# Attention followed by a squared-ReLU feed-forward layer on one core: a two-part start, another route for batch 2, smaller w_out units and another order of exps

## The chip, the cores and the metric

The kernel runs on one core of a Trainium2 chip. The metric is device time in microseconds (us) of one execution. The span that the profile shows is about 1.7 us shorter than that time, because it runs from the first to the last instruction.

## The reference

Eight batches of attention (8 heads, 576 tokens, 64 columns, 16 extra "beacon" keys and values ahead of the tokens, causal among the tokens), then a feed-forward layer over all 4608 tokens:

```python
scores = scale * np.matmul(q, concat([beacon_k, k]).transpose(0, 1, 3, 2))     # masked above the diagonal
a = exp(scores - max); a /= a.sum(-1) + 1e-09
x = np.matmul(a, concat([beacon_v, v])).transpose(0, 2, 1, 3).reshape(4608, 512)
h = x @ w_in                 # 512 x 2048
r = np.maximum(h, 0.0)
return (r * r) @ w_out       # 2048 x 512
```

Inputs and output are fp32; the kernel computes in bf16.

## The kernel before

A small list scheduler inside the kernel fixes, when the kernel is built, the order of instructions on every engine. It guesses durations, and the chip may be slower or faster, but the order stays: if TensorE reaches an instruction whose data is late, everything behind it waits. The same holds for SyncE, on whose queue most loads, all crossbar transposes and all stores stand.

Keys and queries must be transposed (head columns on the partitions). Batches below `NPE` are loaded and cast in one transfer by GpSimd and transposed by TensorE; the others are loaded in natural layout by SyncE, cast by GpSimd, and transposed by a DMA through the crossbar. The attention output `xn` must be transposed too: on TensorE for batches below `NXPE`, by five crossbar transposes on SyncE for the others.

```python
    NPE = 3
    NXPE = 2
    # ...
    def add_strided(b, prio):                     # q and k of batches 0 to 2
        after = [w_ops["in", 3]] if b == 1 else [strided[b - 1][HP - 1, "q"]] if b else []
        step = 1 if b == 0 else 2
        for pr in range(0, HP, step):
            h = slice(2 * pr, 2 * (pr + step))
            for n, (x, t, dst) in enumerate((("k", k, ks), ("q", q, qs))):
                # one load for all 576 tokens of these heads: 96 partitions x 6 tokens
                ... nc.gpsimd.dma_start(out=dst[b % 2][:, h],
                                        in_=t[b, h].rearrange("h (p s) d -> p h s d", s=NS))
    # ... 12 transposes of 96x96 for each pair of heads, for k and for q
    def add_trans(b, x, prio):                    # q or k of batches 3 to 7, on SyncE
        ... nc.sync.dma_start(out=dst[b % 2]..., in_=srcb[b % 2]..., transpose=True)
        deps = [cast[b, x, c] for c in range(NT)]
    # ...
                exps.append(add(..., "ACT", ..., prio=base + i + s, deps=[qk], give=(qk, s)))
    # ...
    def add_xt(b):                                # x of batches NXPE to 7, on SyncE
        for t in range(NT):
            ... nc.sync.dma_start(out=xT[:, :, at:at + n], in_=xn[b % 2][0:n, t, :], transpose=True)
    # ...
    def add_weights():                            # w_in in quarters, behind batch 0's v
            w_ops["in", i] = add(f"win{i}", "POOL", 1.3, emit, prio=-100 + i,
                                 sync=[v_loads[0][3]] if i == 0 else (),
                                 behind=[w_ops["in", i - 1]] if i else (), dma=3.15)
    # ...
            for half in range(2):                 # w_out: 16 matmuls of a 128-token tile in 2 units of 8
                prev = add(f"s2.{j}.{ts}.{half}", "PE", 1.73, emit_s2, ...)
    # ...
        if b < NXPE:
            add_xt_pe(b)
        else:
            add_xt(b)
```

The first batch's attention is split by tokens: the first 240 go through attention and the first w_in matmuls (width 240) before the other 336 (w_in width 272 for what is left of the first chunk of 512).

The softmax here doesn't subtract the row's maximum and nothing guards it: scores larger than these inputs give would overflow.

Of the kernel before, what the change touches and what calls it, by code (L numbers as in the profile page):

```python
# [179 lines left out]
def kernel(  # L180
# [29 lines left out]
    def sb(name, shape, dt):  # L210
# [13 lines left out]
          for i in range(2)]  # L224
    kb = [qk_area[:, (2 * i + 1) * W:(2 * i + 2) * W].rearrange("p (g c d) -> p g c d", g=HP, c=NT)
          for i in range(2)]
    qs = [qk_area[0:NP, (2 * i) * WS:(2 * i + 1) * WS].rearrange("p (h s d) -> p h s d", h=H, s=NS)
          for i in range(2)]
    ks = [qk_area[0:NP, (2 * i + 1) * WS:(2 * i + 2) * WS].rearrange("p (h s d) -> p h s d", h=H, s=NS)
          for i in range(2)]  # L230
    bkf = [sb("bkf", [Nb, H, D], FP32)] * 2
    bks = [sb(f"bks{i}", [Nb, H, D], BF16) for i in range(2)]
    vb = [sb(f"vb{i}", [128, NT, H, D + 1], BF16) for i in range(2)]
# [65 lines left out]
    def t_start(t):  # L299
        return max(0, 128 * t - Nb)  # L300

    NPE = 3
    NXPE = 2
    SOFT_V = (1,)
    zero_ops = {}
    strided = {}
# [66 lines left out]
    def add_beacon(b, prio):  # L373
        ld = add(f"bkl{b}", "SP", 0.65, lambda e: [nc.sync.dma_start(
            out=bkf[b % 2], in_=beacon_k[b].transpose([1, 0, 2]))], prio=prio, dma=0.1,
                 deps=[cast[b - 1, "bk"]] if b else [])
        cast[b, "bk"] = add(f"bkc{b}", "DVE", 0.4, lambda e: nc.vector.tensor_copy(bks[b % 2], bkf[b % 2]), prio=prio,
                               deps=[ld])
        return cast[b, "bk"]

    def add_strided(b, prio):
        loads = {}
        bk = add_beacon(b, prio)
        after = [w_ops["in", 3]] if b == 1 else [strided[b - 1][HP - 1, "q"]] if b else []
        free = trans[b - 2, "q"] + trans[b - 2, "k"] if b >= 2 else []
        trans[b, "q"], trans[b, "k"] = [], []
        step = 1 if b == 0 else 2
        for pr in range(0, HP, step):
            h = slice(2 * pr, 2 * (pr + step))
            for n, (x, t, dst) in enumerate((("k", k, ks), ("q", q, qs))):  # L390
                def emit(e, t=t, dst=dst, h=h):
                    return [nc.gpsimd.dma_start(out=dst[b % 2][:, h],  # L392
                                                in_=t[b, h].rearrange("h (p s) d -> p h s d", s=NS))]
                o = add(f"sld{b}{x}{pr}", "POOL", 0.65 * step, emit, prio=prio + pr + 0.1 * n, behind=after,
                        deps=free, dma=0.92 * step)
                for i in range(step):
                    loads[pr + i, x] = o
        strided[b] = loads
        for pr in range(HP):
            h = slice(2 * pr, 2 * pr + 2)  # L400
            box = {}

            busy = qk_ops[HP * (b - 2) + pr] if b >= 2 else []

            def emit_tp(e, x, pr=pr, h=h, box=box):
                pp = ps[box[x].held[2]].bitcast(BF16)
                t, at = (ks, Nb) if x == "k" else (qs, 0)
                if x == "k":
                    nc.tensor.transpose(pp[:, 0:Nb], bks[b % 2][:, h, :], ident[0:Nb, 0:Nb])  # L409
                for u in range(NS):  # L410
                    for hj in range(2):
                        nc.tensor.transpose(pp[64 * hj:64 * hj + 64, at + u * NP:at + (u + 1) * NP],  # L412
                                            t[b % 2][:, 2 * pr + hj, u, :], ident[0:NP, 0:NP])

            for n, x in enumerate("kq"):
                box[x] = add(f"tp{b}.{pr}{x}", "PE", 0.65 if b else 0.9, lambda e, x=x, f=emit_tp: f(e, x),
                             prio=100.0 * (HP * b + pr) - 190 + 0.1 * n,
                             deps=[bk if x == "k" else None, loads[pr, x], ident_op] + busy, take=("ps", "tp"))

            def emit_k(e, pr=pr, box=box):  # L420
                pp = ps[box["k"].held[2]].bitcast(BF16)
                copy_on(e, kT[b % 2][:, pr, 0:Nb], pp[:, 0:Nb])
                copy_on(e, kT[b % 2][:, pr, Nb:Nb + S].rearrange("p (n s) -> p n s", s=NS),
                        pp[:, Nb:Nb + S].rearrange("p (s n) -> p n s", s=NS))

            def emit_q(e, pr=pr, box=box):
                pp = ps[box["q"].held[2]].bitcast(BF16)
                copy_on(e, qT[b % 2][:, pr, 0:S].rearrange("p (n s) -> p n s", s=NS),
                        pp[:, 0:S].rearrange("p (s n) -> p n s", s=NS))

            ek = add(f"ek{b}.{pr}", "DVE", 0.85, emit_k, prio=-200.0, deps=[box["k"]], give=box["k"])
            eq = add(f"eq{b}.{pr}", ("DVE", "ACT"), 0.7, emit_q, prio=-199.0, deps=[box["q"]], give=box["q"])
            trans[b, "k"].append(ek)
            trans[b, "q"].append(eq)


    class Phase:

# [43 lines left out]
    def add_pair(b, pr):  # L482
        p = HP * b + pr
        qk_ops[p] = []

        def gate(o):
            if p < HP:
                return True
            return o.progress >= mlp_chunk_us * (LEAD + PACE * (p - HP))

        if b < NPE:
            qk_deps = [trans[b, "k"][pr], trans[b, "q"][pr]]
        else:
            qk_deps = trans[b, "k"] + trans[b, "q"]
        take_pt = add(f"pt{p}", "-", 0.0, None, prio=100.0 * p, deps=qk_deps, take=("pt", "pt"), gate=gate)
        av_ops[p] = []
        for n, ph in enumerate(phases(b)):
            add_phase(b, pr, p, n, ph, take_pt, qk_deps, gate)

    def add_phase(b, pr, p, n, ph, take_pt, qk_deps, gate):  # L500
        base = 100.0 * p + 1000.0 * n
# [2 lines left out]
        for i in range(0, len(ph.pieces), size):  # L504
# [22 lines left out]
            for s, (_, off, width) in enumerate(group):  # L527
                def emit_exp(e, off=off, width=width, box=box, s=s):
                    st = strips[box["qk"].slots[s]]
                    nc.scalar.activation(pt[take_pt.held[2]][:, :, off:off + width], st[:, :, 0:width],  # L530
                                         AF.Exp, bias=0.0, scale=scale)

                exps.append(add(f"exp{p}.{n}.{i + s}", "ACT", 0.18 + 2 * width / 1200.0, emit_exp,
                                prio=base + i + s, deps=[qk], give=(qk, s)))

        def emit_mask(e):
            P = pt[take_pt.held[2]]
# [111 lines left out]
    def add_weights():  # L649
        for i in range(4):  # L650
            def emit(e, i=i):
                w = d_ff // 4
                return [nc.gpsimd.dma_start(  # L653
                    out=w_in_sb[:, :, i * w:(i + 1) * w],
                    in_=moe_w_in.rearrange("(m p) f -> p m f", p=128)[:, :, i * w:(i + 1) * w])]
            w_ops["in", i] = add(f"win{i}", "POOL", 1.3, emit, prio=-100 + i, sync=[v_loads[0][3]] if i == 0 else (),
                                 behind=[w_ops["in", i - 1]] if i else (), dma=3.15)
    def add_weights_out():
        for i in range(4):
            def emit(e, i=i):  # L660
# [6 lines left out]
    def add_chunk(j):  # L667
# [52 lines left out]
            sq.append(sqs)  # L720
        for ts in range(TCH // 128):
            prev, first = None, {}
            for half in range(2):
                def emit_s2(e, ts=ts, half=half, first=first):
                    o = ps[first["s2"].held[2]]
                    for fc in range(8 * half, 8 * half + 8):
                        nc.tensor.matmul(o, G[:, fc, ts * 128:(ts + 1) * 128],  # L727
                                         w_out_sb[:, fc, :], start=(fc == 0), stop=(fc == NFT - 1))

                prev = add(f"s2.{j}.{ts}.{half}", "PE", 1.73, emit_s2, prio=base + 100 + 2 * ts + half,  # L730
                           deps=[x for f in range(4 * half, 4 * half + 4) for x in sq[f]]
                           + [w_ops["out", qd] for qd in (2 * half, 2 * half + 1)] + [prev],
                           take=None if half else ("ps", "mlp"), pe_time=1.73)
                first.setdefault("s2", prev)
            s2_ops[j, ts] = prev
            u = 2 * j + ts // 2
# [29 lines left out]
    late = []  # L766
    for b in range(B):
        lp = 10.0 * b
        if b < NPE:
            add_strided(b, lp - 200.0 if b == 0 else lp)  # L770
        if NPE <= b < NPE + 2:
# [2 lines left out]
        for n, (x, c) in enumerate(([] if b < NPE else nat) + [("v", c) for c in range(NT)]):  # L774
            behind, sync = [], []
            if x == "v" and b == 0:
                if c == 0:
                    sync = [strided[0][0, "q"]]
            elif x == "v" and b == 1 and c == 0:
                behind = [strided[1][HP - 1, "q"]]  # L780
            elif b == 2 and n == 0:
                sync = [w_ops["out", 3]]
            add_load(b, x, c, lp + 0.1 * n, behind, sync)
            if x == "v":
                v_loads[b].append(load_chain[-1])
        if b >= NPE:
            add_trans(b, "k", lp - 5.0)
            add_trans(b, "q", lp - 5.1)
        if b == 0:
            add_weights()  # L790
        if b == 1:
            add_weights_out()
        for pr in range(HP):
# [45 lines left out]
```

## Time and profile before

| | before |
|---|---|
| time, median of 3 | 351.12 us (350.99 to 351.77) |
| span in the profile | 349.6 us |
| TensorE busy | 335.9 us, 96% |
| first w_in matmul; first of width 272 | 26.47 us; 34.45 us |
| TensorE at half speed until | about 25.9 us |

These are lines of the page: the span, then each engine's busy time (PE is TensorE, PEld its weight loads, DVE VectorE, ACT ScalarE, POOL GpSimd).

```profile
span 349.6 us, 7413 instructions
PE 335.9 (96%) x2980; PEld 179.5 (51%) x2980; DVE 167.9 (48%) x391; ACT 197.3 (56%) x298; POOL 82.8 (24%) x132
```

The table of windows of the kernel before says where the other 4% lie. After the window's bounds and length come each engine's busy us with its instructions, the granted clock, the DMA engines' share and GB/s.

```profile
core 0: us, PE busy (x) PEld busy (x) DVE busy (x) ACT busy (x) POOL busy (x), PEclk, DMA share, GB/s
0.00:10.00 10.00, 3.73 (x59) 2.56 (x61) 5.66 (x25) 2.82 (x4) 6.82 (x18) 1.00 0.80 113
10.00:20.00 10.00, 7.83 (x97) 4.58 (x97) 5.92 (x20) 6.26 (x9) 3.81 (x6) 1.00 0.72 141
20.00:30.00 10.00, 9.70 (x141) 7.18 (x142) 7.87 (x34) 8.56 (x13) 6.03 (x9) 1.00 1.19 197
30.00:40.00 10.00, 9.18 (x161) 7.01 (x161) 7.14 (x19) 6.65 (x15) 4.77 (x8) 1.00 1.22 216
50.00:100.00 50.00, 50.00 (x567) 27.90 (x566) 32.41 (x75) 33.21 (x48) 17.57 (x30) 1.00 1.17 213
```

TensorE is the limit from 50 us on. It is idle in the first 20 us, where it has little data, and it is slow there too. The timeline of TensorE before shows the speed: start, duration, line, operation, output and inputs, and the number of matmuls. The same 12 attention-value matmuls take 0.84 us at 22.88 and 0.53 us at 27.04, although the clock column reads 1.00 in all the windows above.

```profile
22.88 0.84 PE L563 MATMUL ps<-vb,pt 128*128 128x65 bf16 x12
26.47 0.58 PE L692 MATMUL ps<-xT,w_in 128*128 128x240 bf16 x4
27.04 0.53 PE L563 MATMUL ps<-vb,pt 128*128 128x65 bf16 x12
34.45 1.10 PE L692 MATMUL ps<-xT,w_in 128*128 128x272 bf16 x8
```

The list of DMA issues of the kernel before in the first 50 us (KB each, median us from issue to landing) has the w_in quarters and the last v load of batch 0. Both are quick, since w_in is issued when v has landed.

```profile
w_in<-in_moe_w_in_dram POOLq DMA_DIRECT2D x4, 512.0 KB, 8.3
stg<-in_v_dram SPq DMA_DIRECT2D x1, 160.0 KB, 4.8
```

```profile
152.18 1.03 PE L692 MATMUL ps<-xT,w_in 128*128 128x512 bf16 x4
```

That w_in work needs 320 tokens of batch 3, which are the first three of the five. The third is issued from about 148.15 on (145.57 and twice 1.29); with 2.5 us from the start of its issue to landing (measured below, in e4) it is there at about 150.6. So the kernel before has about 1.5 us in hand here. That is an estimate from these lines, and it was made only after the experiments.

### The profile page before, as it was taken

The page shows a single profiled execution, that of the slowest core. Times are in us where ns is not written, and L with a number is a line of the kernel's source. Part 1 is how long each engine was busy: PE and PEld are TensorE (multiplying, and loading weights), DVE is VectorE, ACT ScalarE, POOL GpSimd, SP SyncE. Part 2 cuts the span into 40 slices and gives each one's busy share as a digit, 9 for nine tenths or more (in the row PEclk, how much of TensorE's full clock was granted, in tenths as well). Part 3 has the DMA queues.
Part 4 walks back from the last instruction along what each step waited for, and adds up shares of the span by engine and source line. Part 5 has one row for each costly group of instructions (what it writes and reads, how often), then busy time and mean ns, then how long its engine had stood idle before and what let it go on. Part 6 is the DMA issues. An engine that isn't in the chain of part 4 may idle for free.

```text
span 349.6 us, 7413 instructions
## 1 busy us (share of the span) xinstructions
PE 335.9 (96%) x2980; PEld 179.5 (51%) x2980; DVE 167.9 (48%) x391; ACT 197.3 (56%) x298; POOL 82.8 (24%) x132
## 2 busy tenths in 40 slices
PE   3789999999999999999999999999999999999995
PEld 2458676645454455444445875454544444444442
DVE  6477886645762576237632864266413302301300
ACT  1686775657834876467646764577436515614611
POOL 7274640472353046105250440000000000000000
PEclk9999999999999999999999999999999999999999
DMA  7989999999998999969996999240015011011002
GB/s 101 185 139 204 220 206 210 217 234 191 230 202 143 215 253 204 187 141 233 218 229 97 220 259 155 86 113 16 2 60 129 0 60 60 2 60 61 2 13 107
DMA packets 137010, 49.50 MB, mean 142 GB/s; under 512 B 123344, under 2 KB 132048, under 8 KB 136976
## 3 DMA queue, kind: packets, MB, share of 16 engines
q1 hardware_dynamic: 127472, 40.09, 55.9%
q0 software_dynamic: 9504, 8.95, 15.7%
q8 instruction: 23, 0.38, 0.5%
q14 instruction: 11, 0.09, 0.1%
HBM read 37.22 MB, written 9.44 MB: 133 GB/s over the span
## 4 chain that ended last, share of the span: by engine, by line
PE 86%; DMA 9%; POOL 1%; SPq 1%; issue 1%; ACT 0%; POOLq 0%; ACTq 0%
PE ps L727 36%; PE ps L692 34%; PE ps L563 8%; PE strip L515 7%; DMA stg<-in_v_dram 5%; DMA qk_area<-in_k_dram 4%; SPq L331 1%; DMA qk_area<-in_q_dram 1%; POOL w_in L653 1%; PE ps L412 1%; POOL vb L286 0%; PE ps L628 0%; ACT osb L284 0%; POOL qk_area L392 0%; PE ps L409 0%
## 5 line engine op out<-in xcount | busy, mean ns | idle before, releaser
L692 PE MATMUL ps<-xT,w_in 128*128 128x512 bf16 (+3 forms) x704 | 134.4, 340 | 0.0
L727 PE MATMUL ps<-w_out,g 128*128 128x512 bf16 x576 | 130.5, 379 | 0.0
L530 ACT ACTIVATE pt<-strip 128x832 bf16<-128x832 f32 (+4 forms) x128 | 104.3, 863 | 37.3 <-PE strip L515 36.9
L708 ACT ACTIVATE g<-ps 128x512 bf16<-128x512 f32 (+2 forms) x126 | 70.3, 558 | 40.9 <-PE ps L692 39.8
L692 PEld LDWEIGHTS <-w_in 128*128 128x128 bf16 x704 | 65.1, 98 | 53.9 <-issue 2.5
L727 PEld LDWEIGHTS <-g 128*128 128x128 bf16 x576 | 54.2, 98 | 63.3 <-issue 1.2
L717 DVE TENSOR_TENSOR g<-g 128x1024 bf16<-128x1024 bf16 (+2 forms) x80 | 52.7, 661 | 59.3 <-ACT g L708 57.6
L284 ACT COPY osb<-ps 128x512 f32<-128x512 f32 x33 | 19.3, 585 | 57.8 <-PE ps L727 57.8
L563 PEld LDWEIGHTS <-pt 128*128 128x128 bf16 (+1 forms) x960 | 37.3, 99 | 17.0 <-issue 8.1
L286 POOL CAST qk_area<-stg 128x512 bf16<-128x512 f32 (+2 forms) x50 | 34.1, 695 | 42.9 <-DMA stg<-in_k_dram 21.6
L563 PE MATMUL ps<-vb,pt 128*128 128x65 bf16 (+1 forms) x960 | 42.6, 197 | 0.7 <-POOL vb L286 0.4
L286 POOL CAST vb<-stg 128x512 bf16<-128x512 f32 (+1 forms) x38 | 24.0, 646 | 66.0 <-DMA stg<-in_v_dram 22.7
L540 DVE TENSOR_TENSOR pt<-pt,tri 128x1024 bf16<-128x1024 bf16 (+1 forms) x36 | 23.9, 669 | 30.2 <-ACT pt L530 30.1
L515 PE MATMUL strip<-qT,kT 64*128 64x80 bf16 (+7 forms) x400 | 37.2, 293 | 0.1
L580 DVE TENSOR_TENSOR xn<-ps,rcp 128x320 bf16<-128x320 f32 (+2 forms) x72 | 32.7, 454 | 2.6
L579 DVE RECIPROCAL rcp<-ps 128x5 f32<-128x5 f32 (+2 forms) x72 | 13.4, 186 | 39.7 <-PE ps L563 39.3
L710 DVE TENSOR_SCALAR g<-ps 128x512 bf16<-128x512 f32 (+2 forms) x34 | 21.0, 620 | 16.9 <-PE ps L692 16.0
L515 PEld LDWEIGHTS <-kT 64*128 64x128 bf16 x400 | 12.9, 97 | 16.7 <-issue 12.7
L412 PE MATMUL ps<-ident,qk_area 96*64 96x96 bf16 x288 | 12.3, 234 | 4.0 <-DMA qk_area<-in_k_dram 2.3
L286 DVE COPY kT<-ps 128x16 bf16<-128x16 bf16 (+1 forms) x24 | 9.8, 454 | 6.8 <-PE ps L412 6.7
L412 PEld LDWEIGHTS <-qk_area 96*64 96x64 bf16 x288 | 8.9, 126 | 6.3 <-DMA qk_area<-in_k_dram 2.7
L544 DVE TENSOR_TENSOR pt<-pt,tri 80x160 bf16<-80x160 bf16 x32 | 10.4, 324 | 0.0
(33 smaller groups left out, 58.1 us busy)
## 6 DMA issues: line engine op xcount, KB each, us to landing
out_dram<-osb SPq DMA_DIRECT2D x17, 512.0 KB, 3.1
stg<-in_v_dram SPq DMA_DIRECT2D x21, 256.0 KB, 5.3
stg<-in_q_dram SPq DMA_DIRECT2D x20, 256.0 KB, 5.0
stg<-in_k_dram SPq DMA_DIRECT2D x15, 256.0 KB, 5.1
w_in<-in_moe_w_in_dram POOLq DMA_DIRECT2D x4, 512.0 KB, 8.3
w_out<-in_moe_w_out_dram POOLq DMA_DIRECT2D x4, 512.0 KB, 11.0
stg<-in_v_dram SPq DMA_DIRECT2D x7, 224.0 KB, 4.8
qk_area<-in_k_dram POOLq DMA_DIRECT2D x4, 288.0 KB, 12.3
```

Of the source, the lines that this page charges most:

```text
L286: eng[e].tensor_copy(dst, src)
L412: nc.tensor.transpose(pp[64 * hj:64 * hj + 64, at + u * NP:at + (u + 1) * NP], t[b % 2][:, 2 * pr + hj, u, :], ident[0:NP, 0:NP])
L515: nc.tensor.matmul(st[:, hj, at:at + t1 - t0], kT[b % 2][hp, pr, 128 * c:128 * c + 128], qT[b % 2][hp, pr, t0:t1], start=True, stop=True,)
L530: nc.scalar.activation(pt[take_pt.held[2]][:, :, off:off + width], st[:, :, 0:width], AF.Exp, bias=0.0, scale=scale)
L540: nc.vector.tensor_tensor(out=d, in0=d, in1=tri[:, m0:m0 + m, :][:, None].to_broadcast([128, 2, m, 128]), op=ALU.min)
L563: nc.tensor.matmul(a[:, (t - tl[0]) * (D + 1):(t - tl[0] + 1) * (D + 1)], P[0:rr, hj, o:o + 128], vb[b % 2][0:rr, c, h, :], start=(c == 0) ...
L580: nc.vector.tensor_tensor(out=xn[b % 2].rearrange("p t (h d) -> p t h d", d=D)[:, tl[0]:tl[0] + nt, h], in0=a[:, :, 0:D], in1=r[:, :, None ...
L692: nc.tensor.matmul(h[:, lo - spans[0][0]:hi - spans[0][0]], w_in_sb[:, mc, ft * 128:(ft + 1) * 128], xT[:, mc, lo % RING:lo % RING + hi - lo],
L708: nc.scalar.activation(dst, h, AF.Relu, bias=0.0, scale=1.0)
L710: nc.vector.tensor_scalar(out=dst, in0=h, scalar1=0.0, scalar2=None, op0=ALU.max)
L717: nc.vector.tensor_tensor(out=d, in0=d, in1=d, op=ALU.mult)
L727: nc.tensor.matmul(o, G[:, fc, ts * 128:(ts + 1) * 128], w_out_sb[:, fc, :], start=(fc == 0), stop=(fc == NFT - 1))
```

## The change

The intent is to fill the empty start and to take work from TensorE.

1. Batch 0's q and k are loaded in two parts (tokens 0 to 239, then the rest), with the first w_in quarter right behind the first part, and the other three behind the second. Three of v's five loads now wait for the first part.
2. Batch 2's q and k leave TensorE for the crossbar (`NPE` 3 to 2), and batch 2's x comes to TensorE in exchange (`NXPE` 2 to 3).
3. w_out is issued in units of 4 matmuls rather than 8.
4. On ScalarE, ready exps go ahead of ready relus.

```diff
+    whole_parts = [(0, NP, NS)]
+    parts_of = {0: [(0, 120, 2), (240, 112, 3)], 1: whole_parts, 2: whole_parts}
@@
-    NPE = 3
-    NXPE = 2
+    NPE = 2
+    NXPE = 3
@@ (add_part_loads is new; add_strided is rewritten to transpose and evict part by part)
+    def add_part_loads(b, part, prio, after, free):
+        t0, np_, ns = parts_of[b][part]
+        step = HP // 2
+        for pr in range(0, HP, step):
+            ...
+                    return [nc.gpsimd.dma_start(
+                        out=strided_buf(b, x, part)[:, h],
+                        in_=t[b, h, t0:t0 + np_ * ns, :].rearrange("h (p s) d -> p h s d", s=ns))]
@@
-                                prio=base + i + s, deps=[qk], give=(qk, s)))
+                                prio=(base + i + s) * 1.0e-4 - 30.0, deps=[qk], give=(qk, s)))
@@
-            w_ops["in", i] = add(f"win{i}", "POOL", 1.3, emit, prio=-100 + i, sync=[v_loads[0][3]] if i == 0 else (),
-                                 behind=[w_ops["in", i - 1]] if i else (), dma=3.15)
+            w_ops["in", i] = add(f"win{i}", "POOL", 1.3, emit, prio=-100 + i, behind=first_loads[min(i, 1)] if i < 2 else [w_ops["in", i - 1]], dma=3.15)
+            if i == 0:
+                first_loads.append(add_part_loads(0, 1, -95.0, [w_ops["in", 0]], []))
@@
-            for half in range(2):
+            for qd in range(4):
                 ...
-                    for fc in range(8 * half, 8 * half + 8):
+                    for fc in range(4 * qd, 4 * qd + 4):
@@
             if x == "v" and b == 0:
-                if c == 0:
-                    sync = [strided[0][0, "q"]]
+                if c == 2:
+                    sync = [strided[0, 0, HP - 1, "q"]]
```

Cut: the grouping of the 4 beacon transposes of a batch into one unit, and the bookkeeping of buffers.

## The prediction

> **What bounds the kernel.** TensorE: busy 335.9 of 349.6 us on the page (96%); the table of windows shows it 100% busy from 50 to 262 us and 83.86 of 84 us after that. Idle time lies at the start: 6.3 us in 0:10, 2.2 in 10:20, 1.5 in 20:50; the last 3.6 us are the final eviction and store. The start also runs at half speed: in the timeline 12 attention-value matmuls take 0.84 us at 22.9 us and 0.53 at 27.0; 12 q/k transposes 0.69 us at 10 us and 0.45 at 33.6. The switch falls at about 25.9 us. The Trainium skill ("TensorE: Matmul & The Clock Gate", Part 1) says the array starts at half clock until sustained activity releases it; the durations agree, though the page's clock row says 9 throughout.
>
> **What changes, with slots (start to start) from the timeline after 50 us.**
> - Batch 2's q/k leave TensorE: 8 groups of 12 transposes at 0.38 us plus 4 beacon transposes at 0.1: -3.4 us. Its x comes on: 4 groups of 5 at about 0.3 us: +1.3. Batch 0 has 16 transposes fewer: -0.5. My sum of all TensorE slots, with other small differences, falls from 328.1 to 326.0 us. All on the critical path.
> - w_out units of 4, and exps before relus, only reorder: a w_out matmul's slot is 0.216 us either way, and after 50 us there is no wait to remove. About 0.
> - Batch 2's q/k need 10 natural loads (256-byte rows, about 900 packets/us, 10.5 us), casts and two crossbar transposes of 5 to 7 us. Ready near 68 us; TensorE asks near 76. No stall.
> - Start. Before: w_in is issued at 18.1 behind the v loads, the DMA engines idle from 17 to 19.5, its first quarter lands at 26.5, and the first w_in matmul follows at once. After: tokens 0 to 239 are in by 9 us, w_in's first quarter by 13. But in TensorE's order the first w_in matmul stands behind all transposes of the second part, which queues behind that quarter and shares the DMA engines with v: landing 14 to 19 us (estimate). So first w_in matmul near 20 us. ScalarE then has 12 exps of 0.87 us plus copies, until about 29 us as before; TensorE fills with w_in work, half of it still at half clock.
>
> **Sum.** Before, the first w_in matmul of width 272 starts at 34.5 us. After, it stands 3.9 us of work deeper; I expect it at 36.8 us (34.5 to 38.5, by when the clock rises: 19, 22.5 or 26 us), with 304.6 + 3.6 us to follow. So the start gains 1.5 us, later waits 0.5 to 1, batch 2's exchange 2. Span about 345.5, time **347.0 us**, range 342.5 to 350.5. Faster by over 2% (below 344.2): 0.2; within 2%: 0.76; slower: 0.04.
>
> **What would show it.** First w_in matmul at 18 to 22 us; TensorE idle before 20 us still 6 to 8 us; half-speed durations until 22 to 26 us; last exp of batch 0 at 28 to 30 us; no TensorE idle from 50 to 340 us; batch 2's crossbar transposes landed before its first qk.
>
> **What would make it wrong.** A denser start may lift the clock at 19 us: 2 to 3 us better. The first part's 512-byte reads may be slower[...]: no gain at the start. Batch 2's crossbar transposes may land after 76 us, as all queues share 16 DMA engines ("DMA: Bandwidth & Descriptors", Issuing engines are not separate DMA queues; no run here shows it yet), and stall TensorE, whose order is fixed.

## More of the kernel before

The timeline of SyncE before, near 140 us, shows the crossbar transposes of batch 5's q and k and then of batch 3's x: each holds the queue for as long as its duration says. TensorE's timeline has the first w_in matmuls on that x.

```profile
137.55 4.16 SPq L363 DMA_TRANSPOSE qT<-qk_area  x1
141.80 3.68 SPq L363 DMA_TRANSPOSE kT<-qk_area  x1
145.57 6.44 SPq L611 DMA_TRANSPOSE xT<-xn  x5
```

## The result, and the profile after

Ratios are the mean time of one kernel's fast runs over that of the other's fast runs of the same rounds, so they are not quite the ratios of the medians quoted beside them.

| | before | after |
|---|---|---|
| time, median of 4 | 351.44 us (350.99 to 351.86) | 355.83 us (354.81 to 356.42) |
| ratio | 1 | 1.0122, 95% interval 1.0094 to 1.0151 |
| span in the profile | 349.6 us | 354.3 us |
| TensorE busy | 335.9 us | 331.6 us |
| first w_in matmul | 26.47 us | 21.76 us |
| first w_in matmul of width 272 | 34.45 us | 45.42 us |
| from there to the end | 315.2 us | 308.9 us |

The change made the kernel 1.2% slower; the prediction was 1.2% faster. The same views of the kernel after follow: the page, the waits of TensorE (what was waited for: us in total, times, longest), and the table of windows.

```profile
span 354.3 us, 7194 instructions
PE 331.6 (94%) x2846; PEld 176.9 (50%) x2884; DVE 172.9 (49%) x396; ACT 191.2 (54%) x287; POOL 89.2 (25%) x137
```

```profile
PE ps L725 <- DVE xT L292: 7.0, 1, 7.0
```

```profile
0.00:10.00 10.00, 1.86 (x24) 1.25 (x24) 4.47 (x24) 2.11 (x4) 8.74 (x19) 1.00 0.93 124
10.00:20.00 10.00, 9.15 (x114) 5.65 (x114) 8.14 (x30) 6.95 (x12) 6.62 (x10) 1.00 1.34 188
20.00:30.00 10.00, 2.99 (x31) 1.62 (x28) 1.12 (x5) 2.92 (x5) 3.25 (x4) 1.00 1.23 196
30.00:40.00 10.00, 10.00 (x136) 7.15 (x135) 8.00 (x25) 7.05 (x11) 6.59 (x10) 1.00 1.17 216
50.00:100.00 50.00, 49.45 (x440) 27.35 (x444) 30.04 (x66) 29.53 (x46) 19.56 (x27) 1.00 1.04 192
```

The window from 20 to 30 us is nearly empty on TensorE, VectorE and ScalarE, while the DMA engines are as busy as anywhere. The timelines of TensorE and then of VectorE after say why. In brackets stand the idle time before an instruction and what ended it.

```profile
21.76 0.78 PE L725 MATMUL ps<-xT,w_in 128*128 128x240 bf16 x3
29.55 0.36 PE L725 MATMUL ps<-xT,w_in 128*128 128x240 bf16 x1 [7.01 <-DVE xT L292]
31.01 0.84 PE L595 MATMUL ps<-vb,pt 128*128 128x65 bf16 x12
34.82 0.53 PE L595 MATMUL ps<-vb,pt 128*128 128x65 bf16 x12
45.42 1.10 PE L725 MATMUL ps<-xT,w_in 128*128 128x272 bf16 x8
```

```profile
28.88 0.43 DVE L292 CAST vb<-stg 80x512 bf16<-80x512 f32 x1 [8.95 <-DMA stg<-in_v_dram]
29.22 0.27 DVE L292 COPY xT<-ps 128x240 bf16<-128x240 bf16 x1
```

TensorE waits for a copy on VectorE, the copy stands in VectorE's fixed order behind the cast of the last v tile, and that cast waits for the load of v. A wait named after one engine was a late DMA. The chain of waits (start, us, what) and the list of DMA issues agree: the last v load takes 18.2 us from the start of its issue to landing, where it took 4.8 in the kernel before (and 9.7 in e1 below, the fairer comparison, where it is issued as early but w_in is held back).

```profile
10.67 18.18 DMA stg<-in_v_dram
```

```profile
w_in<-in_moe_w_in_dram POOLq DMA_DIRECT2D x4, 512.0 KB, 12.8
stg<-in_v_dram SPq DMA_DIRECT2D x1, 160.0 KB, 18.2
```

The DMA view of the kernel after from 18 to 26 us shows how the two shared the engines. Its columns are the queue, packets, MB, and the share of the 16 engines' time. q0 carries w_in (issued by GpSimd), q1 carries v (issued by SyncE).

```profile
q0 software_dynamic: 1242, 1.24, 91.1%
q1 hardware_dynamic: 1239, 0.31, 29.8%
```

The packets are equal in number and not in size: 1 KB for w_in, 256 bytes for v (as the profile counts them). While both are queued, as many packets of one move as of the other, and a w_in packet has four times the size, so v gets a fifth of the bytes: 155 of its packets in a us. By itself v moves about 1000 in a us (e1, from 18 to 19 us: 1000, beside 49 of q0). The three late loads hold 672 KB, which is 2688 such packets, and their time has three parts. They are issued from 9.5 us on, but none of their packets moves before 13.0 us; why is not shown, and it is about the same in e1. From 14 to 17 us they move 285 in a us, in turn with the 384-byte packets of q and k's second part (854 against 848). From 18 to 27 us they move 155 in a us, beside w_in. The Trainium skill ("DMA: Bandwidth & Descriptors", Queues, rings and completion order) says that each DMA engine takes turns between the queues it has work for, packet by packet. The trace agrees, 1242 against 1239; since a packet in the page's sense can hold several of the rows counted here, equal counts don't show how many go in one turn. I had read that section and cited its neighbour, and had not drawn this conclusion from it.

After 60 us TensorE has no wait over 0.23 us. The remainder of the kernel, from the first 272-wide w_in matmul to the end, takes 308.9 us, where the prediction's sum had 308.2. So nearly the whole miss of the profiled run is in its first 45 us. That alone would be a simple story, and the experiments show that it is not the whole of it.

### The profile page after: what moved, and what is told of

It reads as the page before. It is cut to its first block, busy times and chain, and to the rows that moved or that the text cites. A ratio compares the mean times of both kernels' runs of the same rounds, so it can differ in the third digit from the quotient of the medians.

```text
span 354.3 us, 7194 instructions
## 1 busy us (share of the span) xinstructions
PE 331.6 (94%) x2846; PEld 176.9 (50%) x2884; DVE 172.9 (49%) x396; ACT 191.2 (54%) x287; POOL 89.2 (25%) x137
## 4 chain that ended last, share of the span: by engine, by line
PE 85%; DMA 9%; DVE 3%; issue 1%; POOL 1%; SPq 0%; ACT 0%; DVEq 0%; ACTq 0%; POOLq 0%
PE ps L760 35%; PE ps L725 33%; PE ps L595 8%; PE strip L547 7%; DMA stg<-in_v_dram 5%; DMA kT<-qk_area 2%; DMA qk_area<-in_q_dram 1%; DVE g L750 1%; PE ps L660 1%; PE ps L443 1%; POOL qk_area L411 1%; DVE xn L612 1%; DVE g L743 0%; SPq L337 0%; DVE pt L572 0%
## 5 line engine op out<-in xcount | busy, mean ns | idle before, releaser
L725 PEld LDWEIGHTS <-w_in 128*128 128x128 bf16 x704 | 65.9, 98 | 56.2 <-issue 3.8
L750 DVE TENSOR_TENSOR g<-g 128x1024 bf16<-128x1024 bf16 (+2 forms) x80 | 54.2, 680 | 73.5 <-ACT g L741 71.8
L741 ACT ACTIVATE g<-ps 128x512 bf16<-128x512 f32 (+2 forms) x118 | 67.6, 573 | 41.3 <-PE ps L725 39.3
L760 PEld LDWEIGHTS <-g 128*128 128x128 bf16 x576 | 53.0, 98 | 60.6 <-issue 2.4
L292 POOL CAST qk_area<-stg 128x512 bf16<-128x512 f32 (+2 forms) x60 | 40.7, 684 | 41.2 <-DMA stg<-in_k_dram 24.4
L290 ACT COPY osb<-ps 128x512 f32<-128x512 f32 x25 | 14.6, 585 | 55.1 <-PE ps L760 54.4
L572 DVE TENSOR_TENSOR pt<-pt,tri 128x1024 bf16<-128x1024 bf16 (+1 forms) x36 | 24.5, 679 | 10.1 <-ACT pt L562 9.8
L743 DVE TENSOR_SCALAR g<-ps 128x512 bf16<-128x512 f32 (+2 forms) x42 | 23.7, 567 | 10.8 <-PE ps L725 9.9
L292 DVE COPY osb<-ps 128x512 f32<-128x512 f32 x11 | 7.6, 691 | 16.7 <-PE ps L760 14.8
L443 PE MATMUL ps<-ident,qk_area 96*64 96x96 bf16 (+2 forms) x176 | 8.9, 251 | 3.5 <-DMA qk_area<-in_k_dram 1.9
L290 ACT COPY qT<-ps 128x240 bf16<-128x240 bf16 (+2 forms) x9 | 3.7, 428 | 11.1 <-DVE kT L292 8.6
```

The lines of the kernel that those rows point to most:

```text
L290: nc.scalar.copy(dst, src)
L292: eng[e].tensor_copy(dst, src)
L572: nc.vector.tensor_tensor(out=d, in0=d, in1=tri[:, m0:m0 + m, :][:, None].to_broadcast([128, 2, m, 128]), op=ALU.min)
L725: nc.tensor.matmul(h[:, lo - spans[0][0]:hi - spans[0][0]], w_in_sb[:, mc, ft * 128:(ft + 1) * 128], xT[:, mc, lo % RING:lo % RING + hi - lo],
L741: nc.scalar.activation(dst, h, AF.Relu, bias=0.0, scale=1.0)
L743: nc.vector.tensor_scalar(out=dst, in0=h, scalar1=0.0, scalar2=None, op0=ALU.max)
```

## The experiments

Eighteen runs were made, all with correct outputs, and all in the fast state but for e6, a single execution whose state is unknown. In the diffs, B stands for the kernel before and A for the one after. The kernel before moves by itself: its medians in the six sets of runs, each on another chip, were 353.06, 351.61, 352.26, 351.56, 352.04 and 352.02 us, so each ratio is taken to the kernel before of its own set.

One caution holds for all of them: the scheduler sorts the queues anew for every edit. On SyncE, batch 3's x stands ahead of batch 5's q and k in A and e1, between them in e4, and behind both in the kernel before, e3, e5, e7 and e9. So no edit changes one thing alone.

| run | start | batch 2's q, k | x on TensorE | order parts | ratio to before, 95% |
|---|---|---|---|---|---|
| after | two-part | crossbar | 0, 1, 2 | yes | 1.0122 (1.0094 to 1.0151) |
| e1 | repaired | crossbar | 0, 1, 2 | yes | 1.0100 (1.0058 to 1.0142) |
| e2 | two-part, cast moved | crossbar | 0, 1, 2 | yes | 1.0107 (1.0075 to 1.0140) |
| e3 | two-part | TensorE | 0, 1 | yes | 1.0119 (1.0084 to 1.0153) |
| e4 | before | crossbar | 0, 1, 2 | no | 1.0183 (1.0149 to 1.0216) |
| e5 | repaired | TensorE | 0, 1 | yes | 1.0062 (1.0028 to 1.0096) |
| e7 | before | TensorE | 0, 1 | yes | 1.0070 (1.0038 to 1.0103) |
| e8 | before, useless matmuls | TensorE | 0, 1 | no | 1.0017 (0.9977 to 1.0057) |
| e9 | repaired | TensorE | 0, 1 | no | 0.9988 (0.9923 to 1.0054) |
| e10 | repaired | TensorE | 0, 1, 2, 3 | yes | 1.0000 (0.9971 to 1.0028) |
| e11 | before | crossbar | 0, 1, 2, 3 | no | 1.0016 (0.9992 to 1.0041) |
| e12 | repaired | crossbar | 0, 1, 2, 3 | yes | 1.0037 (1.0010 to 1.0064) |
| e13 | before | TensorE | 0, 1, 2, 3 | yes | 1.0048 (1.0025 to 1.0071) |
| e14 | repaired | TensorE | 0, 1, 2, 3 | no | 1.0008 (0.9985 to 1.0030) |
| e15 | repaired, useless matmuls | TensorE | 0, 1, 2, 3 | no | 1.0003 (0.9977 to 1.0029) |
| e16 | before | TensorE | 0, 1, 2, 3 | no | 1.0036 (1.0011 to 1.0062) |
| e17 | before | TensorE | 0, 1, 2, 3 | w_out only | 1.0043 (1.0020 to 1.0066) |
| e18 | repaired | TensorE | 0, 1, 3 | no | 0.9980 (0.9952 to 1.0008) |

### e1: let batch 0's v land before the second w_in quarter

My theory after the result was that the 7 us at the start are the whole loss. This is the "repaired" start of the table.

```diff
 # from A
+        if b == 0:
+            w_ops["in", 1].need.append(v_loads[0][4])
+            w_ops["in", 1].sync.append(v_loads[0][4])
         if b == 1:
             add_weights_out()
```

> The changed kernel with one wait added: the second w_in quarter is issued only once the last v load of batch 0 has landed. Theory (v starved: the last three v loads of batch 0 share the DMA engines packet for packet with w_in's quarters 2 to 4 and land at 25 to 28.5 us; TensorE waits 7 us for them and stays at half clock until about 34 us): the last v load lands by 18 us, TensorE's idle time in 20:30 falls from 7 us to under 1.5, the first w_in matmul of width 272 starts at 36 to 38.5 us instead of 45.4, and the time is 346 to 349 us, below before. Rival (the two-part loads or the other parts are what costs): time stays above 353 us. A second theory, that batch 2's crossbar transposes come next: TensorE then waits 2 to 5 us at the first qk of batch 2 near 78 us, and the time is 348 to 351 us.

Measured: 356.65 us, ratio 1.0100, where I had expected a time below the kernel before. The last v load lands at 20.2 us rather than 28.9. The wait at the start is gone, and the first 272-wide w_in matmul starts at 37.30 us rather than 45.42. The row of the table of windows:

```profile
20.00:30.00 10.00, 10.00 (x126) 6.83 (x124) 7.27 (x26) 7.78 (x12) 7.51 (x11) 1.00 0.93 145
```

But from there to the end the kernel takes 317.9 us instead of 308.9. The waits of TensorE after 100 us in this run are new:

```profile
PE strip L547 <- DMA kT<-qk_area: 3.3, 2, 2.3
PE ps L725 <- DMA xT<-xn: 2.1, 1, 2.1
```

They make 5.4 of the 9.0 us. Lost clock makes most of the rest: the clock column has 0.87 from 100 to 110 us, 0.96 from 110 to 120 and 0.66 from 155 to 160, which is 3.4 us of work at full speed (an estimate from these three numbers), and the durations agree (15 attention-value matmuls take 1.03 us at 108.14 and 0.62 at 99.60).

So the late v was the cause of the 7 us, and it was not the whole loss: an eight-microsecond-earlier TensorE runs into loads and crossbar transposes of later batches, which in the kernel after had time to catch up during the stall. Batch 3's x, for one, was ready at 138.1 us and stood on SyncE behind loads until 148.71.

### e2: is it the load, or the place of the cast on VectorE?

```diff
 # from A
-        engs = ("POOL", "DVE") if b == 0 else ("POOL",)
+        engs = ("POOL", "DVE") if b == 0 and c < 4 else ("POOL",)
```

> The changed kernel with the cast of the last v tile of batch 0 on GpSimd instead of VectorE, nothing else moved. Theory (the load lands late; attention-value work of the second part needs it right after): TensorE still waits, 6 to 7.5 us in 20:30, time 354 to 357 us. Rival (the load's lateness would be harmless, but the cast stands ahead of the x eviction in VectorE's order and blocks it): the 7 us go, time 347 to 350 us.

Measured: 357.11 us, ratio 1.0107, and the wait has only changed its name, 3.62 us before the attention-value matmuls at 26.55 and 3.42 at 30.40:

```profile
PE ps L595 <- POOL vb L292: 7.0, 2, 3.6
```

The rival, that the copy merely stood at a bad place in VectorE's order, falls. The load was late: it landed at 29.69 us, and GpSimd cast it from 29.74 on.

### e3: the change without batch 2's exchange

```diff
 # from A
-    NPE = 2
-    NXPE = 3
+    NPE = 3
+    NXPE = 2
```

> The changed kernel with batch 2 as in before: q/k by strided loads and TensorE transposes, x by crossbar. Theory (the exchange of batch 2 itself gains TensorE's slots, about 2 us, and the loss is at the start): TensorE waits 7 us in 20:30 as in the changed kernel, time 357 to 359 us. Rival (the exchange costs): time below 355 us.

Measured: 357.47 us, ratio 1.0119. The wait at the start is 4.5 us here rather than 7.0, with more waits for q and k before it, and no wait of TensorE over 0.2 us comes later. With the stall at the start in place, the exchange makes no difference that could be seen (1.0119 against 1.0122, from different sets). That fits e1: the stall hides what comes later.

### e4: batch 2's exchange alone, on the kernel before

```diff
 # from B
-    NPE = 3
-    NXPE = 2
+    NPE = 2
+    NXPE = 3
```

> The kernel before with the exchange of batch 2 alone. Theory: start as in before, TensorE's slots fall by 2.3 us, no wait above 1 us at batch 2's first qk near 79 us: time 348.5 to 350 us. Rival (the crossbar transposes of batch 2 come too late): a wait of 2 to 5 us at that qk, time 351 to 354 us.

Measured: 359.57 us, ratio 1.0183. The part that was to gain 2 us loses 6.4 us alone. The wait that the rival named, at batch 2's first qk, was only 0.7 us. The profile of e4 shows one long wait of TensorE, then the queue of SyncE around it, and then the table of windows:

```profile
PE ps L692 <- DMA xT<-xn: 7.4, 1, 7.4
```

```profile
142.81 3.96 SPq L331 DMA_DIRECT2D stg<-in_v_dram  x4
146.88 4.24 SPq L363 DMA_TRANSPOSE qT<-qk_area  x1
151.21 6.44 SPq L611 DMA_TRANSPOSE xT<-xn  x5
```

```profile
150.00:155.00 5.00, 0.00 (x0) 0.00 (x0) 0.00 (x0) 0.00 (x0) 0.88 (x2) 0.82 0.73 157
155.00:160.00 5.00, 3.69 (x23) 1.52 (x25) 0.00 (x0) 1.76 (x3) 0.00 (x0) 0.50 0.58 146
160.00:165.00 5.00, 4.87 (x42) 2.38 (x41) 3.73 (x8) 2.96 (x5) 0.00 (x0) 0.99 0.98 203
```

Batch 3's x was ready to be transposed at 135.0 us (the end of its last normalization, which starts at 134.53), but stood behind batch 5's q in SyncE's order. That q's own casts had ended by 143.4, but it stood in turn behind loads of k and v, which SyncE issued until 146.77; a load needs a free staging tile, and those come free as GpSimd casts earlier loads. The chain of waits of e4 goes through three loads before it reaches x:

```profile
133.43 5.40 DMA stg<-in_q_dram
139.79 3.77 DMA stg<-in_k_dram
143.94 5.55 DMA stg<-in_v_dram
153.78 2.48 DMA xT<-xn
```

(The chain's step from the third of these loads to q's transpose is the profile's inference: the program makes that transpose wait for no v, and it was on the queue from 146.88.) In the kernel before the same transposes of x began at 145.57, here at 151.21. The loads are later, it seems, because batch 2's q and k now pass through the same queue and the same GpSimd casts as those of batches 3 to 5. What the runs show is that batch 5's q is transposed from 146.9 or 147.0 us on with the exchange (e4, e11, e12), and from between 137.6 and 142.4 without it (the kernel before, e3, e5, e7, e9, e14); A and e1 can't be compared, since x goes first there. The stall also cost the clock: it is 0.50 from 155 to 160 us. The Trainium skill ("TensorE: Matmul & The Clock Gate", Part 1) says that an idle stretch of about 3.4 us puts the array back to half clock; after 7.4 us without work this run agrees. Shorter waits were enough in e1, where the clock fell after 2.3 and 2.2 us; in e12 it stayed at 1.00 through two waits of 2.1 us.

### e5: repaired start and no exchange

```diff
 # from A
+            w_ops["in", 1].need.append(v_loads[0][4])
+            w_ops["in", 1].sync.append(v_loads[0][4])
@@
-    NPE = 2
-    NXPE = 3
+    NPE = 3
+    NXPE = 2
```

> The changed kernel with both repairs: second w_in quarter behind batch 0's last v load, and batch 2 back on TensorE as in before. Theory (two costs that hide each other: v landing late at the start, and batch 2's loads and crossbar transposes making batches 3 to 5 late): neither wait is left, TensorE idles under 1.5 us in all after 20 us, the clock is not lost again, and the time is 0.5 to 2 us below before (ratio 0.994 to 0.999), since the two-part start itself gains under 1 us. Rival (something else in the change costs, in the two-part loads or in the order): ratio above 1.003.

Measured: 353.78 us, ratio 1.0062. I expected no waits; there was one of 3.71 us for x at 152.78. Here too batch 3's x (issued at 147.44) stands behind batch 5's q and k. So the exchange is not needed for that wait. TensorE asked for x at 149.07, 3.1 us earlier than in the kernel before (152.18), and x's transposes began 1.9 us later; the kernel before had only about 1.5 us in hand.

### e6: the kernel before, unchanged

> The kernel before, unchanged, for its profile on this chip. If it runs near 351 us: no TensorE wait over 0.3 us after 50 us, as in its first profile. If it runs near 353 us as on the chip of the last four runs: TensorE waits of 1 us or more for loads or transposes after 60 us, which would show that before has no slack left on the DMA side.

Measured in one look: 350.71 us, span 349.0, no wait of TensorE of 0.3 us or more after 38 us. The 2.3 us of e7 below are not in it.

### e7: the order parts alone

```diff
 # from B
-            for half in range(2):
+            for qd in range(4):              # w_out in units of 4 matmuls, as in A
@@
-                                prio=base + i + s, deps=[qk], give=(qk, s)))
+                                prio=(base + i + s) * 1.0e-4 - 30.0, deps=[qk], give=(qk, s)))
```

> The kernel before with two parts of the change alone: w_out units of 4 matmuls and exps ahead of relus on ScalarE. Theory (they only reorder): within 1 us of before, ratio 0.997 to 1.003. Rival (they cost or gain by themselves): outside of that.

Measured: 354.26 us, ratio 1.0070, where about 0 was predicted. TensorE's waits after 40 us are for batch 3's x again, whose transposes began at 146.58 rather than 145.57, while TensorE asked for it at 150.71 rather than 152.18:

```profile
PE ps L692 <- DMA xT<-xn: 2.3, 2, 1.2
```

### e8: raise the clock in the kernel before

```diff
 # from B
+    dum = g[1][:, 0, :]
+    nc.vector.memset(dum, 0.5)
+    for _ in range(8):
+        nc.tensor.matmul(strips[0][:, 0, :], dum[:, 0:128], dum, start=True, stop=True)
@@ (behind each group of batch 0's transposes, into the unused half of its bank)
+                    for _ in range(3):
+                        nc.tensor.matmul(ps[box[x].held[2]][:, 300:512], dum[:, 0:128], dum[:, 0:212], start=True, stop=True)
```

> The kernel before with useless matmuls on TensorE: 8 of width 512 before the first load has landed, and 3 of width 212 behind each of batch 0's transpose groups. Theory (at the start the array runs at half clock until 26 us for want of activity, which costs 7 to 8 us of TensorE time): the full clock comes by 10 to 16 us, 12 attention-value matmuls before 24 us take 0.53 us instead of 0.84, and the time falls by 2 to 5 us (ratio 0.986 to 0.994), less than 7 because data and ScalarE then set the pace. Rival (the half speed has another cause, such as operands or waits): durations before 26 us unchanged, time equal or 1 us longer.

Measured: 352.31 us, ratio 1.0017. The clock did rise: 12 transposes took 0.45 us near 5 us, where they take 0.69 us near 10 us in the kernel before. Then it fell again, and stayed at half from 12 to 24 us, so the first 272-wide w_in matmul came at 34.70 us, no sooner than before. The mechanism is there; this way of using it bought nothing.

### e9: the repaired start alone

```diff
 # from e5: the order parts of B again
-            for qd in range(4):
+            for half in range(2):            # w_out in units of 8 matmuls, as in B
@@
-                                prio=(base + i + s) * 1.0e-4 - 30.0, deps=[qk], give=(qk, s)))
+                                prio=base + i + s, deps=[qk], give=(qk, s)))
```

> The two-part start alone, repaired: batch 0 in two parts, first w_in quarter right behind the first part, the other quarters behind batch 0's last v load; batch 2, w_out units and ScalarE order as in before. Theory (the repaired start gains about 1 us at the first w_in matmul of width 272, and nothing else moves): ratio 0.994 to 0.999 if the loads of batches 3 to 5 keep up, and TensorE has no wait above 0.5 us between 60 and 340 us. Rival (before has under 2 us of slack at batch 3's x near 152 us, so an earlier start only runs into it): a wait of 1 to 3 us for x's crossbar transposes near 150 us with the clock lost for some us behind it, ratio 0.999 to 1.008.

Measured: 351.03 us, ratio 0.9988 with an interval of 0.9923 to 1.0054. Three executions lay at 350.69 to 351.27 us and one, the profiled one, at 355.74, with waits of 2.0 and 1.0 us for crossbar transposes of x. It decides nothing by itself; it says that x sits near an edge.

### e10, e11, e12: take batch 3's x from SyncE's queue

If x is late because it stands on SyncE's queue, it can be tested without touching any wait: TensorE transposes batch 3's x too. The Trainium skill ("DMA: Bandwidth & Descriptors", Silent corruption: two transposing streams in flight at once) rules out the other way, a second queue for crossbar transposes, unless each waits for the other to complete. No run here tried it.

```diff
 # e10: from A with e1's and e3's lines      e11: from B with NPE = 2     e12: from A with e1's lines
-    NXPE = 2                      # or 3
+    NXPE = 4
```

> The changed kernel with v first, batch 2's q/k on TensorE, and the x of batches 2 and 3 on TensorE, so that the first x by crossbar is batch 4's. Against the run that had v first and all of batch 2 as in before (ratio 1.006, a wait of 3.7 us for batch 3's x at 153 us and clock lost behind it). Theory (that wait comes from the sync engine's queue, where x stands behind q/k transposes that wait for v casts and loads): the wait at 150 to 155 us goes, TensorE has 2 us more work, ratio 1.000 to 1.004. Rival (TensorE has simply run ahead of all loads): the wait comes back within 20 us for another load or transpose, ratio 1.005 or more.

> The kernel before with batch 2's exchange, and batch 3's x on TensorE too. The exchange alone took ratio 1.018, with a wait of 7.4 us for batch 3's x at 156 us and half clock until about 161 us. Theory (x stuck on the sync engine's queue behind q/k transposes of batch 5): that wait goes and with it 8 to 10 us, against 1 us more work: ratio 0.993 to 1.001. Rival (the loads themselves are late): waits of 3 us or more for q/k transposes of batches 4 and 5 take its place, ratio 1.006 to 1.016.

> The changed kernel with v first and batch 3's x on TensorE too; batch 2's q/k stay on the crossbar. With v first alone: ratio 1.010, waits of 2.3 us at 106 and 1.0 us at 134 us for k's crossbar transposes and 2.2 us at 154 us for batch 3's x. Theory (late k is due to batch 2's loads, late x to the sync engine's queue): the wait for x goes, those for k stay at 2 to 4 us in all, ratio 1.002 to 1.008. Rival (one cause for all): all three go or all three stay.

Measured: e10 352.33 us, ratio 1.0000, no wait of TensorE of 0.3 us or more after 40 us. It is e5 with this one step, and 0.6% better (different sets, intervals that only touch) although TensorE has some 2.6 us more work (the prediction's 1.3 us for one batch's x, twice). e11 353.30 us, ratio 1.0016, just above the range that I expected: it is e4 with this step, and 1.7% better; the 7.4 us wait is gone, and 1.4 us of waits for crossbar transposes of k remain. e12 353.83 us, ratio 1.0037: the wait for x is gone, 4.9 us of waits for k remain, one of them in each of three batches. The waits of e10 and then of e12:

```profile
PE ps L595 <- POOL vb L292: 0.2, 1, 0.2
PE strip L547 <- DMA kT<-qk_area: 4.9, 3, 2.1
```

So x was late because of the queue, and k is late because of batch 2's extra loads: without the exchange (e10) k is in time.

### e13, e16, e17: what do the order parts cost by themselves?

```diff
 # e13: e7 with batch 3's x on TensorE     e17: e13 without the exps' rank     e16: B with this line alone
-    NXPE = 2
+    NXPE = 4
```

> The kernel before with the order parts of the change alone (w_out in units of 4 matmuls, exps ahead of relus), as in e7, but batch 3's x is transposed by TensorE as well as batch 2's, so that no x waits on the crossbar there. Theory (e7's 0.7% is the wait for batch 3's x behind the q/k transposes on SyncE's queue): no TensorE wait for xT of a DMA over 0.5 us after 100 us; some 2.6 us more TensorE work; ratio to the kernel before 0.999 to 1.005, below e7's 1.007. Rival (the small w_out units or the exps' order themselves cost time): the waits are gone and the ratio is still 1.007 to 1.014.

> The kernel before with one change of its own: batches 2 and 3 have their x transposed by TensorE, as in e10, e13 and e14, nothing else. It is the base that e13 and e14 have to be held against. Theory (the extra TensorE work of some 2.6 us is paid in full, since TensorE is the limit, and the repaired two-part start and the order parts are worth about as much where they come with it): ratio 1.003 to 1.008, no new wait of TensorE; then the order parts cost nothing by themselves (e13 1.0048) and the repaired start is worth 0.2 to 0.7% (e14 1.0008). Rival (x on TensorE is nearly free, because it takes crossbar work off the sync queue): ratio 0.998 to 1.002; then the start is worth nothing and the order parts cost 0.3 to 0.6% by themselves.

> e13 without the exps' new rank: the kernel before with x of batches 2 and 3 on TensorE and w_out in units of 4 matmuls. Theory (if the order parts cost time by themselves, it is the exps put ahead of the relus, which holds up the first batch's relus and so the first w_in work): ratio within 0.002 of e16's and 0.002 or more below e13's. Rival (the small units cost it, or neither does): ratio within 0.002 of e13's.

Measured: e16 353.44 us, ratio 1.0036; e17 353.62 us, 1.0043; e13 353.55 us, 1.0048. None has a wait for x. e16 is the base of the other two: x of two batches more on TensorE costs 0.36% by itself, and the order parts add 0.12% to it at most, which the intervals don't tell from nothing. So e7's 0.7% is the wait for x (2.3 us, which is 0.65%), not the order itself. e13 alone would have misled: its 1.0048 looks like a cost of the order until e16 gives the base.

### e14, e18: what is the repaired start worth?

```diff
 # e14: e9 with NXPE = 4      e18: e14 with
-        if b < NXPE:
+        if b < 2 or b == 3:
```

> The two-part start with the repair (second w_in quarter behind batch 0's last v load), order and batch 2's q/k as before, as in e9, but with batch 3's x on TensorE. Theory (e9's slow execution and its waits of 2.04 us near 155 us come from x on the crossbar; the repaired start is worth under 1 us): no TensorE wait over 0.5 us after 50 us, the executions lie within 0.5% of each other, ratio 0.997 to 1.002. Rival (the start is worth the 2 us or more that the prediction gave it): ratio 0.994 or less.

> e14 (repaired two-part start, the rest as before) with only batch 3's x on TensorE; batch 2's x goes back to the crossbar, where no run has shown a wait for it. Theory (TensorE work is paid in full, and the repaired start is worth some 0.3%): 1.3 us less TensorE work than e14, no TensorE wait over 0.5 us after 50 us, ratio 0.994 to 0.999, so that this version beats both kernels. Rival (a wait for batch 2's x near 105 us takes its place, or the clock falls once): ratio 0.999 to 1.004.

Measured: e14 351.82 us, ratio 1.0008, executions from 351.44 to 352.92, no wait over 0.6 us. Against e16 (1.0036) the repaired start is worth about 0.3%, 1 us; the two ratios come from different calls and their intervals overlap, so this size is likely and not shown. The two groups of executions that e9 had are gone, as expected. e18 351.20 us, ratio 0.9980 with an interval of 0.9952 to 1.0008: TensorE lacks only 0.04 busy us between 50 and 262 us. This is the best kernel, and its gain over the kernel before, about 0.7 us, is not outside the noise.

### e15: the repaired start with a full clock

```diff
 # from e14
+    for _ in range(12):
+        nc.tensor.matmul(strips[0][:, 0, :], dum[:, 0:128], dum, start=True, stop=True)
@@ (behind each group of transposes of the first part)
+                                for _ in range(10 if (pr, x) == (0, "k") else 3):
+                                    nc.tensor.matmul(ps[box["t"].held[2]][:, 256:512], dum[:, 0:128], dum[:, 0:256], start=True, stop=True)
```

> e14 with useless matmuls that keep TensorE busy in the first 20 us (12 of width 512 at once, 10 of width 256 behind the first k transposes, 3 behind the other first-part transposes). Theory (the half clock of the start lasts until TensorE has been busy for long enough without a gap; the two-part start has its w_in work early and can use the full clock): the 12-transposes units take 0.45 us rather than 0.69 before 20 us and the first w_in matmul of width 272 starts 2 to 6 us earlier than in e14; ratio 0.985 to 0.998. Rival (as in e8 the clock rises and falls back in the gaps, or the loads and not the clock set the pace): the first 272-wide matmul starts within 1.5 us of e14's and the ratio is within 0.003 of e14's.

Measured: 351.37 us, ratio 1.0003. This time the clock stayed up: the timeline of TensorE has 12 second-part transposes in 0.49 us where e14 has 0.77, and the first w_in unit in 0.58 us where e14 has 0.98. Yet the first 272-wide w_in matmul starts at 38.51 us, in e14 at 38.50. The table of windows shows what holds both back, first in e14 and then in e15:

```profile
20.00:30.00 10.00, 10.00 (x142) 6.65 (x139) 7.53 (x26) 8.74 (x15) 7.43 (x11) 1.00 0.94 149
20.00:30.00 10.00, 9.61 (x161) 6.69 (x162) 8.59 (x32) 9.96 (x17) 6.64 (x10) 1.00 0.96 147
```

In e15 the useless matmuls delayed the second part's transposes from 14.92 to 17.33 us; the full clock then made the delay good, until ScalarE was busy for 9.96 of 10 us with exps and relus. From 24.5 us on the two kernels run side by side. So the half clock is not what keeps the two-part start from gaining more. Whether a full clock without the useless work would help is open; ScalarE leaves little room.

## Why the prediction was wrong, point by point

**The start, "which queues behind that quarter and shares the DMA engines with v: landing 14 to 19 us (estimate)": the step that failed.** The sum knew that v and w_in would share, and gave a landing time for the second part of q and k only; those were about in time (landed at 13.5 to 18.1 us; first w_in matmul at 21.76 us, predicted 18 to 22). It gave none for v, and it did not ask what sharing does to a queue of small packets. v's last load took 18.2 us (9.7 in e1, where w_in is held back) and held VectorE, then TensorE, for 7.0 us. e1 takes the wait away by moving w_in's quarters, e2 shows that the cast's place doesn't matter. The predicted start of the first 272-wide matmul was 36.8 us, with the stall it was 45.42, without it (e1) 37.30. So the term was right but for the wait.

**"half-speed durations until 22 to 26 us": wrong as a consequence.** After the stall the half speed lasted until about 34 us (12 attention-value matmuls still take 0.84 us at 31.01). By difference, with the 7.0 us it makes up the 8.6 us between 36.8 and 45.42. The last exp of batch 0, expected at 28 to 30 us, moved to about 39 us.

**"batch 2's exchange 2", and for its transposes "No stall": right in the work, wrong in the worth.** The sum of the work held (308.9 us from the first 272-wide matmul on, with hardly a wait, where it had 308.2). The first qk of batch 2 did not wait, but by luck: its k landed at 80.5 us, not near 68, and TensorE, held up at the start, asked only at 86.43; in e4 and e12 it asked earlier and waited 0.7 us. Above all, the prediction asked only whether batch 2 itself would be in time. Its loads and casts push those of batches 3 to 5, and through SyncE's order batch 3's x. Alone the exchange costs 1.8% (e4). With x out of the way it gives at best 0.2% (e11 against e16, intervals overlap), and on the repaired start it costs 0.4% (e12 against e10). In the kernel after this loss did not show, because the stall at the start let the loads catch up: with the same order on SyncE but without the stall, e1 has the waits. Two faults, and only one of them was visible in the profile.

**"w_out units of 4, and exps before relus, only reorder", worth "About 0": right by itself, wrong in this kernel.** Alone they cost 0.7% (e7), but through the wait for batch 3's x, not through themselves (e13 and e17 against e16). That "after 50 us there is no wait to remove" was true, and it overlooked that a wait may be added: about 1.5 us of reserve is no wait and can't be seen in a list of waits.

**"the start gains 1.5 us": not contradicted, for the repaired start.** e14 against e16 puts it at 1 us. e18 gains 0.7 us over the kernel before and pays for one more batch of x on TensorE, 0.6 us if that is half of what e16 paid, so 1.3 us (an estimate). Neither is outside the noise.

**"no TensorE idle from 50 to 340 us": right**, within 0.23 us for each wait after 60 us, but only because the stall at the start had given the loads time.

The prediction had named a late crossbar transpose as a risk, for batch 2's own transposes. The same risk came true in e4 and e7, for batch 3's x. What stays open: the true worth of the repaired start (below the noise of these rounds) and whether a better order on SyncE, with x ahead of q and k and of their loads, would keep the exchange's 2 us; that needs another rank for the transposes and was not run (in e1 x stands ahead of q and k but behind loads, and TensorE still waited 2.1 us for it).

## What to carry to other kernels

When a change starts a large transfer earlier, ask what else is in flight then, and compare packet sizes: here the transfer with small packets lost (155 of them in a us instead of about 1000), and it was the one to let land first. Before moving work to an in-order queue, list what stands behind it for the next batches and how much reserve each has, since a reserve of 1 or 2 us shows in no list of waits. When one stall explains the whole loss, take it away and look again: a stall gives later loads time, and it may hide a second fault as large as itself.

## What the Trainium skill lacked or had wrong

- "DMA: Bandwidth & Descriptors", Queues, rings and completion order: taking turns by packet is right (1242 against 1239 packets in 8 us), but it doesn't say what follows when packet sizes differ. Here the 256-byte queue got 0.31 MB and the 1 KB queue 1.24 MB in the same 8 us, and a load of 160 KB took 18.2 us where it took 9.7 in e1, without w_in beside it.
- "DMA: Bandwidth & Descriptors", DMA Transpose (X-bar): the section has nothing on how long the issuing queue is held (a table for trn3 on the same page gives cycle counts of earlier chips, at other sizes). Here one transpose of a batch's q or k held SyncE's queue for 2.9 to 6.1 us over all runs (4.2 and 3.7 in the lines of the kernel before), and five of x for 6.4 us or more, with all other loads and stores waiting behind.
- "TensorE: Matmul & The Clock Gate", Part 1: about 3.4 us of sustained activity is to release the clock. In the kernel before half speed lasted until 25.9 us, with TensorE busy for 7.83 of 10 us from 10 to 20. The page has no number for how dense the activity must be, and the busy share alone doesn't give one: in e8 the clock fell after a window of 2.96 busy us of 4, and in e15 it stayed up through one of 2.77 of 4.
- The same page, on the way back to half clock: in e1 it came after waits of 2.3 and 2.2 us, in e12 not through two of 2.1 us (see e4).
- No page says that the clock column of a profile can read 1.00 during the first half-speed stretch, as it does in both kernels here until 25.9 and 34 us; durations have to be compared. The page just named does warn that records of clock changes are not to be trusted without a cross-check. After a later stall the column was right (0.50 in e4).
